# Moving the places at which SyncE hands over loads, in an attention kernel with a gated convolution

## Chip, cores, metric

The kernel runs on one core of a Trainium2 chip. The metric is the device time of one execution in microseconds (us), lower is better. Here PE is TensorE's matmuls and PEld its weight loads, DVE is VectorE, ACT ScalarE, POOL GpSimd and SP SyncE, which hands loads to the DMA engines.

## What is computed

For 8 batches of 8 heads there are 512 local and 32 global positions with head size 64. Global queries attend to all positions; a local query attends to the global ones and to local ones at most 32 away. The heads are joined into rows of 512, and a gated block follows: a causal convolution over 5 positions makes a gate, `w_val` a value, and `w_out` is applied to their product.

```
s_g  = scale * q_g @ k_all.T;            out_g = softmax(s_g) @ v_all
s_ll = where(|i - j| <= 32, scale * q_l @ k_l.T, -1e9)
out_l = softmax(concat(scale * q_l @ k_g.T, s_ll)) @ v_all
x = concat(out_g, out_l) as rows of 512
gate = sigmoid(sum_k conv_w[k] * x shifted by 4 - k)
out = (gate * (x @ w_val)) @ w_out
```

## The kernel before

Work is cut into 32 units of two heads (four units a batch). For unit u: `s` makes the scores of 16 blocks of 32 queries against 128 keys each (L521), `mx` masks them and takes the maximum (DVE), `exp` is on ACT, `t` transposes on PE (L554 or L262), `tc` copies to SBUF, `av` multiplies by v (L573), `eps` and `norm` divide, `xt` transposes again (L600 or L262), and `tap` and `conv` make the gate. `gs`, `gmax`, `gexp`, `gt`, `gav`, `gx` do the same for the global queries of a batch (L424, L476, L498). Of a batch, `g1` (L705) multiplies by `w_val` and `g2` (L733) by `w_out`, each matrix split in a high and a low part, so three matmuls of 512 columns for each step `g1.b.e.t` or `g2.b.r.e`. `w0` to `w7` are the weights' 128-row pieces, split in steps `s0` to `s7` on ACT and DVE.

The order of everything is written out by hand in one text, `ORDER` (L52 on): names in the order in which instructions are put into the program; a name's engine takes them in that order. Three kinds of names in it are loads on SyncE: `iqN` (q and k of unit N, 624 KB, L348), `ivN` (v of unit N, 975 KB) and `wiN` (weight piece, 512 KB). SyncE takes them in the order of the text, one queue.

A load's place matters beyond its rank in that queue. `on_pe` notes each TensorE instruction as it is put down, and `transfer` makes the load wait for the last one noted:

```
    def on_pe(ins):
        last_pe[:] = [ins.ins]

    def transfer(out, in_):
        ins = nc.sync.dma_start(out, in_).ins
        if last_pe:
            tc.add_manual_dep(ins, last_pe[0].name, after, reason="a load's place in the line")
```

So a load is handed to the DMA engines when the TensorE work named ahead of it has ended. There are four buffers for q/k and four for v; a load also waits for its buffer's last reader. The first thirteen loads (`FIRST`) are handed over at the start and aren't in `ORDER`.

Of the kernel before, what the change touches and what calls it, by code (L numbers as in the profile page):

```python
# [69 lines left out]
g1.0.3.2 sig3 exp8.1 eps7:ACT iv8 gv.0.2 g1.0.3.3 xt6T@4 norm7 gl.0.1 gv.0.3 gh.0.2:ACT t8@01 w7.s2 w7.s3 xc4:ACT  # L70
xc6:ACT tc8.0:ACT xt5T@6 w6.s7 gs2@24 xc5:ACT iv9 gmax2.0 gh.0.3:ACT gx1@0 gxc1:ACT w7.high:ACT w7.s4 g2.0.0.0@6 gmax2.1
gexp2.0 s9@07 w7.s5 w7.s6 gl.0.3 s10@23 iv11 tap6:ACT tc8.1:ACT gt2.0T@4 gl.0.2 xt7@1 g2.0.0.1 tap5:ACT w7.s7 xc7:DVE
xh7:ACT gtc2.0 tap4:DVE g2.0.0.2 g2.0.0.3 g2.0.1.0@1 g2.0.1.1 g2.0.1.2 ob.0.0:ACT tap7:ACT mx10.0 iq12 xl7 halo7:ACT
gexp2.1 g2.0.1.3 g2.0.2.0@2 g2.0.2.1 ob.0.1:ACT halo4:DVE av8@5 xh4:POOL gav2.0@1 conv4.0 xh6:ACT mx9.0 exp9.0 mx9.1
s11@07 xl4 conv4.1 iq13 xh5:DVE mx10.1 exp9.1 gt2.1T@3 g2.0.2.2 g2.0.2.3 iq14 eps8:DVE exp10.0 norm8 t9@56 mx11.0
halo5:DVE mx11.1 exp10.1 iq15 gtc2.1 tc9.1:DVE ob.0.2:ACT t10@04 gav2.1 tc9.0:ACT tc10.0:ACT conv4.2 av9@5 xl5
tc10.1:ACT geps2:ACT av10@3 gnorm2 st.0.1 gx2@1 g2.0.3.0@0 eps9:ACT conv5.0 conv4.3 eps10:ACT exp11.1 gxc2:ACT norm10
g2.0.3.1 g2.0.3.2 g2.0.3.3 exp11.0 xt8T@1 t11@73 xc8:ACT xl6 ob.0.3:ACT norm9 s12@65 iv14 conv5.1 conv5.2 tc11.0:ACT
s13@24 conv5.3 xt9@7 conv7.0 g1.1.0.0@0 mx13.0 exp13.0 iv12 g1.1.0.1 g1.1.0.2 g1.1.0.3 halo6:ACT xc9:ACT xh9:ACT mx13.1
mx12.0 mx12.1 sig4 gv.1.0 gs3@16 iq16 s14@05 exp12.0 gmax3.0 st.0.3 tc11.1:ACT halo8:DVE av11@3 xt10@1 gexp3.0 eps11:ACT  # L80
mx14.0 iv13 conv7.1 g1.1.1.0@0 iq17 norm11 g1.1.1.1 xc10:ACT tap8:ACT conv6.0 gmax3.1 exp12.1 g1.1.1.2 gt3.0T@3 conv6.1
gtc3.0 iv15 conv7.2 xt11T@6 t12@12 mx14.1 sig5 exp14.0 s15@34 tc12.1:DVE tc12.0:ACT g1.1.1.3 g1.1.2.0@2 conv6.2 exp13.1
gexp3.1 g1.1.2.1 gv.1.1 mx15.0 iq18 conv7.3 g1.1.2.2 conv6.3 g1.1.2.3 xc11:ACT g1.1.3.0@7 g1.1.3.1 mx15.1 sig6 exp14.1
gv.1.2 sig7 av12@3 gh.1.1:DVE st.0.2 gav3.0@0 gt3.1T@1 t13@65 gh.1.0:DVE eps12:DVE norm12 st.0.0 t14@34 gtc3.1 gl.1.0
# [957 lines left out]
```

## Time and profile before

| | before |
|---|---|
| three runs, median | 355.54 us (355.24 to 357.9) |
| profiled execution, its own time | 355.0 us |
| its span, first to last instruction | 353.2 us |
| mean granted TensorE clock | 0.990 |
| TensorE busy (matmuls) | 335.6 us, 95% of the span |
| VectorE busy | 309.0 us, 87% |
| ScalarE busy | 224.8 us, 64% |
| DMA queue of the loads (q1) | 57.01 MB |
| DMA queue of instructions (q8) | 52 packets, 0.85 MB |

The span is the part of the profiled execution from its first to its last instruction; 1.8 us lie around it. Times in the rows are counted from the span's start. "issue" as the cause of idle time means that the engine waited for nothing that the profile shows. Matmul ends are modelled, so a piece of the chain can start a few tenths after the last matmul did. A window counts the instructions that start in it.

### The profile page before, as it was taken

The page shows a single profiled execution, that of the slowest core. Times are in us where ns is not written, and L with a number is a line of the kernel's source. Part 1 is how long each engine was busy: PE and PEld are TensorE (multiplying, and loading weights), DVE is VectorE, ACT ScalarE, POOL GpSimd, SP SyncE. Part 2 cuts the span into 40 slices and gives each one's busy share as a digit, 9 for nine tenths or more (in the row PEclk, how much of TensorE's full clock was granted, in tenths as well). Part 3 has the DMA queues.
Part 4 walks back from the last instruction along what each step waited for, and adds up shares of the span by engine and source line. Part 5 has one row for each costly group of instructions (what it writes and reads, how often), then busy time and mean ns, then how long its engine had stood idle before and what let it go on. Part 6 is the DMA issues. An engine that isn't in the chain of part 4 may idle for free.

```text
span 353.2 us, 15341 instructions
## 1 busy us (share of the span) xinstructions
PE 335.6 (95%) x6658; PEld 269.3 (76%) x6658; DVE 309.0 (87%) x1035; ACT 224.8 (64%) x579; POOL 13.6 (4%) x23
## 2 busy tenths in 40 slices
PE   5889899999799999999999999999999999999994
PEld 2547678778577788788887878887888888888893
DVE  3799999999949999999999998899688898897981
ACT  2779799778728795965965458737876504434221
POOL 4014110001000000000000000000000000000000
PEclk9899999999989999999999999999999999999999
DMA  7987779674719936944494338543580110012124
GB/s 241 413 347 257 264 252 375 228 262 182 248 35 371 341 110 222 371 144 150 130 338 151 140 124 301 199 127 126 183 320 19 55 38 30 2 59 89 60 91 149
DMA packets 17107, 66.64 MB, mean 189 GB/s; under 512 B 1808, under 2 KB 3984, under 8 KB 17040
## 3 DMA queue, kind: packets, MB, share of 16 engines
q1 hardware_dynamic: 12240, 57.01, 45.6%
q10 hardware_dynamic: 4800, 8.65, 6.5%
q8 instruction: 52, 0.85, 0.9%
q14 instruction: 15, 0.12, 0.1%
HBM read 56.74 MB, written 8.91 MB: 186 GB/s over the span
## 4 chain that ended last, share of the span: by engine, by line
PE 88%; ACT 3%; DVE 3%; issue 2%; DMA 2%; ACTq 0%; SPq 0%
PE psum L705 27%; PE psum L733 26%; PE psum L521 9%; PE psum L573 9%; PE psum L262 7%; PE psum L476 3%; DMA qk<-in_qk_dram 2%; PE psum L600 2%; PE psum L424 2%; PE psum L554 2%; PE psum L677 1%; DVE wa L232 1%; ACT pm L540 1%; DVE wraw L232 1%; PE psum L498 1%
## 5 line engine op out<-in xcount | busy, mean ns | idle before, releaser
L232 DVE SCALAR_TENSOR_TENSOR gate<-xc,cw,gate 128x512 f32<-128x512 f32 x120 | 87.6, 750 | 1.0
L540 ACT ACTIVATE pm<-pm,mx 128x128 f32<-128x128 f32 x256 | 80.0, 392 | 9.4 <-DVE mx L232 9.4
L232 DVE CUSTOM_DVE_ANT_0 pm<-psum,small 128x128 f32<-128x128 f32 x256 | 57.8, 285 | 14.3 <-PE psum L521 14.2
L733 PE MATMUL psum<-wol,gh 128*128 128x512 f32 x128 | 50.8, 397 | 3.2 <-issue 3.2
L733 PE MATMUL psum<-woh,gh 128*128 128x512 f32 x128 | 52.1, 407 | 0.0
L705 PE MATMUL psum<-xh,wvh 128*128 128x512 f32 x128 | 52.1, 407 | 0.0
L733 PE MATMUL psum<-woh,gl 128*128 128x512 f32 x128 | 50.6, 395 | 0.0
L705 PE MATMUL psum<-xh,wvl 128*128 128x512 f32 x128 | 50.1, 392 | 0.0
L705 PE MATMUL psum<-xl,wvh 128*128 128x512 f32 x128 | 49.9, 390 | 0.0
L521 PE MATMUL psum<-qk 64*32 64x128 f32 x2048 | 36.5, 277 | 3.3 <-DMA qk<-in_qk_dram 3.3
L689 ACT ACTIVATE gate<-gate 128x512 f32<-128x512 f32 x32 | 19.8, 630 | 29.9 <-DVE gate L232 29.9
L521 PEld LDWEIGHTS psum<-qk 64*32 64x32 f32 x2048 | 29.3, 107 | 9.5 <-DMA qk<-in_qk_dram 5.2
L573 PE MATMUL psum<-v,pts 128*32 128x65 f32 x2048 | 34.5, 221 | 2.0 <-issue 1.8
L573 PEld LDWEIGHTS psum<-v,pts 128*32 128x32 f32 x2048 | 30.5, 110 | 7.3 <-issue 2.8
L330 ACT COPY pts<-psum 128x512 f32<-128x512 f32 x53 | 29.6, 585 | 5.6 <-DVE mx L232 2.4
L733 PEld LDWEIGHTS psum<-wol,gh 128*128 128x128 f32 x128 | 24.5, 191 | 8.1 <-issue 3.6
L733 PEld LDWEIGHTS psum<-woh,gh 128*128 128x128 f32 x128 | 24.7, 193 | 5.2 <-DVE gm L232 0.2
L733 PEld LDWEIGHTS psum<-woh,gl 128*128 128x128 f32 x128 | 24.5, 191 | 5.3
L705 PEld LDWEIGHTS psum<-xh,wvh 128*128 128x128 f32 x128 | 24.0, 188 | 5.8 <-DVE gv L232 0.3
L705 PEld LDWEIGHTS psum<-xh,wvl 128*128 128x128 f32 x128 | 24.0, 188 | 5.5 <-issue 0.3
L705 PEld LDWEIGHTS psum<-xl,wvh 128*128 128x128 f32 x128 | 24.1, 188 | 4.6 <-issue 0.2
L232 DVE SCALAR_TENSOR_TENSOR gv<-gate,psum 128x512 f32<-128x512 f32 x32 | 21.8, 683 | 5.5 <-PE psum L705 3.3
(124 smaller groups left out, 516.4 us busy)
## 6 DMA issues: line engine op xcount, KB each, us to landing
v<-in_vw_dram SPq DMA_DIRECT2D x32, 975.0 KB, 5.5
qk<-in_qk_dram SPq DMA_DIRECT2D x32, 624.0 KB, 5.3
out_dram<-ob ACTq DMA_DIRECT2D x32, 256.0 KB, 2.3
wraw<-in_w_val_dram SPq DMA_DIRECT2D x4, 512.0 KB, 12.1
wraw<-in_w_out_dram SPq DMA_DIRECT2D x4, 512.0 KB, 4.7
out_dram<-obg SPq DMA_DIRECT2D x4, 64.0 KB, 1.7
out_dram<-obg ACTq DMA_DIRECT2D x4, 64.0 KB, 2.0
small<-in_mask_dram SPq DMA_DIRECT2D x1, 148.0 KB, 3.3
```

Source lines behind the costliest of these rows:

```text
L232: ins = made(*args, **kwargs)
L262: on_pe(T.matmul(out, in_, ident[D * r:D * r + D, D * r:D * r + D], is_transpose=True, **more))
L330: A.copy(out, in_)
L424: on_pe(T.matmul(s[h][SG * c:SG * c + SG, cols], qkt[rows, SL + SG * h:SL + SG * h + SG], keys, start=True, stop=True))
L476: on_pe(T.matmul(ag[SG * c:SG * c + SG, :], pgt[:k, s, SG * c:SG * c + SG], vt[:k, w, h, :], start=(n == 0), stop=(n == len(steps) - 1)))
L521: on_pe(T.matmul((sx, sy)[h][32 * j:32 * j + 32, i, :], qkt[rows, 32 * m:32 * m + 32], qkt[rows, k0:k0 + P], start=True, stop=True))
L540: A.activation(out=pm[:, h, i, :], in_=pm[:, h, i, :], func=AF.Exp, bias=mx[:, c:c + 1], scale=-1.0)
L554: on_pe(T.transpose(pt[:, i, :], pm[:, h, i, :], ident))
L573: on_pe(T.matmul(ax[32 * j:32 * j + 32, h, E1 * i:E1 * i + E1], q, vt[:, block_win(4 * i + j), h, :], start=True, stop=True))
L689: A.activation(out=g, in_=g, func=AF.Tanh, scale=0.5)
L705: on_pe(T.matmul(box["pv", e], w[:, e, t * P:t * P + P], x, start=(t == 0 and q == 0), stop=(t == NDT - 1 and q == 2)))
L733: on_pe(T.matmul(box["po", r], g[:, e, rs], w[:, e, :], start=(e == 0 and q == 0), stop=(e == NDT - 1 and q == 2)))
```

## The change

Only `ORDER` changes. It holds 60 names of loads (`iq`, `iv`, `wi`), and 47 of them now stand at another place against TensorE's work: 22 earlier, 25 later. The names of all other work stand in the same order as before, so no instruction of PE, DVE, ACT or POOL is added, removed or moved against another of its engine. Some loads are now handed over together, and SyncE's own order changes in places. As an example, two lines of the text before and the lines that hold the same loads now:

```diff
-gav1.0@2 exp6.0 mx7.0 av5@4 iq10 sig0 gv.0.0 gt1.1@16 mx7.1 conv2.2 conv3.2 sig1 eps5:ACT exp7.0 norm5 gtc1.1 g1.0.1.2
-g1.0.1.3 t7.0@0 conv2.3 exp7.1 iq11 g1.0.2.0@1 w6.s0:ACT w6.s1 tc7.0:ACT gv.0.1 gh.0.0:ACT w6.s2 g1.0.2.1 t7.1@6 t6@54
+conv2.3 exp7.1 g1.0.2.0@1 w6.s0:ACT wi7 w6.s1 tc7.0:ACT iq10 gv.0.1 gh.0.0:ACT w6.s2 g1.0.2.1 t7.1@6 t6@54 conv3.3 w6.s3
+s8@03 tc6.1:ACT gav1.1 tc7.1:ACT av7@6 iq11 gh.0.1:ACT mx8.0 tc6.0:ACT sig2 mx8.1 iv10 geps1:DVE av6@4 w6.s4 w7.s0:ACT
```

Of the loads spoken of below, the TensorE work ahead of each (what it waits for), before and now:

| load | before, behind | now, behind |
|---|---|---|
| iv6, iv5, iv7 | pc1.4, g1.0.0.2, t4.0 | av2, s5, gs1 |
| iq10 | av5 | g1.0.2.0 |
| iq11 | t7.0 | av7 |
| iq13, iq14, iq15 | s11, g2.0.2.3, t9 | g2.0.1.2, g2.0.1.2, s11 |
| iq16, iv13 | gs3, xt10 | s14, t12 |
| iq27 | g1.3.1.1 | g1.3.3.3 |

SyncE's own queue, in the part from v7 or v5 (first row) to v10 (last row). `v_` and `qk_` are the buffers of a v or q/k load, `wraw_` that of a weight piece; the number behind a name counts what was made ahead of it in the program; the brackets name what the load waits for (PE: its place; DMAHW: an earlier transfer that shared its semaphore; Activation, DVE: its buffer). Before: v5, q/k 8, w6, w7, q/k 9, q/k 10, q/k 11, v10.

```order
L348 DMA v_956<-in_vw_dram 128x1950 [waits DMAHW6_49,PE_49]
L348 DMA qk_962<-in_qk_dram 128x1248 [waits DMAHW7_49]
L348 DMA wraw_1025<-in_w_out_dram 128x1024 [waits DMAHW0_49,PE_49,Activation_49]
L348 DMA wraw_1067<-in_w_out_dram 128x1024 [waits DMAHW1_49,DVE_49,PE_49]
L348 DMA qk_1072<-in_qk_dram 128x1248 [waits DMAHW2_49]
L348 DMA qk_1141<-in_qk_dram 128x1248 [waits DMAHW3_49,PE_49]
L348 DMA qk_1186<-in_qk_dram 128x1248 [waits DMAHW4_49,PE_49]
L348 DMA v_1319<-in_vw_dram 128x1950 [waits DMAHW5_49,PE_49]
```

Now v7, w6, q/k 8, q/k 9, w7, q/k 10, q/k 11, v10:

```order
L348 DMA v_902<-in_vw_dram 128x1950 [waits DMAHW6_49,PE_49]
L348 DMA wraw_1004<-in_w_out_dram 128x1024 [waits DMAHW7_49,PE_49,Activation_49]
L348 DMA qk_1016<-in_qk_dram 128x1248 [waits DMAHW0_49,PE_49]
L348 DMA qk_1137<-in_qk_dram 128x1248 [waits DMAHW1_49,PE_49]
L348 DMA wraw_1187<-in_w_out_dram 128x1024 [waits DMAHW2_49,PE_49,Activation_49]
L348 DMA qk_1191<-in_qk_dram 128x1248 [waits DMAHW3_49]
L348 DMA qk_1311<-in_qk_dram 128x1248 [waits DMAHW4_49,PE_49]
L348 DMA v_1324<-in_vw_dram 128x1950 [waits DMAHW5_49]
```

w7 has moved behind q/k 9; where no PE stands in the brackets, the load has the same place as the one ahead of it.

The same queue at the third of the places, from q/k 12 to v14. Before:

```order
L348 DMA qk_1625<-in_qk_dram 128x1248 [waits DMAHW1_49,PE_49]
L348 DMA qk_1750<-in_qk_dram 128x1248 [waits DMAHW2_49,PE_49]
L348 DMA qk_1779<-in_qk_dram 128x1248 [waits DMAHW3_49,PE_49]
L348 DMA qk_1818<-in_qk_dram 128x1248 [waits DMAHW4_49,PE_49]
L348 DMA v_2032<-in_vw_dram 128x1950 [waits DMAHW6_49,PE_49]
```

Now:

```order
L348 DMA qk_1586<-in_qk_dram 128x1248 [waits DMAHW1_49,PE_49]
L348 DMA qk_1619<-in_qk_dram 128x1248 [waits DMAHW2_49,PE_49]
L348 DMA qk_1629<-in_qk_dram 128x1248 [waits DMAHW3_49]
L348 DMA qk_1752<-in_qk_dram 128x1248 [waits DMAHW4_49,PE_49]
L348 DMA v_1958<-in_vw_dram 128x1950 [waits DMAHW6_49,PE_49]
```

The order is the same; each number is smaller, so each load stands further ahead in the program, and q/k 14 has the place of q/k 13.

## Rows read from the trace of the kernel before

**Rows 1.** The page's first part: span, then each engine's busy time.
```profile
span 353.2 us, 15341 instructions
PE 335.6 (95%) x6658; PEld 269.3 (76%) x6658; DVE 309.0 (87%) x1035; ACT 224.8 (64%) x579; POOL 13.6 (4%) x23
```
**Rows 2.** Chain that ended last, in order of time: start us, us, what.
```profile
39.79 0.95 issue
...
41.51 1.08 PE psum L521 x64
...
51.23 1.04 PE psum L573 x64
...
65.33 0.87 issue
66.20 1.90 PE psum L573 x107
...
78.95 6.16 PE psum L733 x27
...
91.69 1.82 PE psum L573 x128
...
94.69 3.21 issue
97.90 3.68 PE psum L733 x8
...
199.18 5.66 PE psum L705 x24
...
211.00 1.15 PE psum L424 x32
```
**Rows 3.** Timeline of DVE and PE: start us, us, engine line op, [idle before <-releaser].
```profile
104.60 0.29 DVE L232 CUSTOM_DVE_ANT_0 pm<-psum,small 128x128 f32<-128x128 f32 x1 [5.08 <-PE psum L521]
...
115.11 0.21 PE L262 MATMUL psum<-ident,pm 64*128 64x64 f32 x1 [0.34 <-issue]
```
**Rows 4.** Windows: us, busy of PE, PEld, DVE, ACT, POOL, clock, DMA, GB/s.
```profile
40.74:66.20 25.46, 24.59 (x638) 19.45 (x637) 24.64 (x102) 22.78 (x60) 1.75 (x2) 1.00 0.83 303
66.20:97.90 31.70, 28.49 (x764) 23.13 (x765) 30.08 (x106) 24.01 (x67) 1.75 (x2) 1.00 0.64 219
97.90:115.11 17.21, 16.87 (x382) 13.10 (x383) 11.54 (x56) 10.55 (x27) 0.00 (x0) 0.90 0.60 216
115.11:162.69 47.58, 47.58 (x1277) 39.15 (x1276) 45.39 (x173) 36.10 (x96) 0.00 (x0) 1.00 0.61 221
...
66.19:85.10 18.91, 18.89 (x379) 15.11 (x383) 18.07 (x62) 14.06 (x34) 1.75 (x2) 1.00 0.66 228
```
**Rows 5.** DMA queues over the span: queue, kind, packets, MB, share of 16 engines.
```profile
q8 instruction: 52, 0.85, 0.9%
```
**Rows 6.** Timeline of SyncE's queue: start of the first, time to the last's end.
```profile
57.02 4.18 SPq L348 DMA_DIRECT2D qk<-in_qk_dram  x3
...
87.87 3.00 SPq L348 DMA_DIRECT2D qk<-in_qk_dram  x3
```
**Rows 7.** DMA queues from 91.3 to 95.4 (q10, the stores, left out).
```profile
q1 hardware_dynamic: 257, 1.17, 87.2%
```
**Rows 8.** DMA queues from 95.4 to 96.5: the queue of instructions.
```profile
q8 instruction: 1, 0.02, 5.2%
```
**Rows 9.** DMA from 97.9 to 98.95, then the queue from 98.95 to 100.
```profile
DMA packets 0, 0.00 MB, mean 0 GB/s; under 512 B 0, under 2 KB 0, under 8 KB 0
...
q8 instruction: 1, 0.02, 5.7%
```
**Rows 10.** Window behind the third stop, columns as in rows 4.
```profile
98.00:101.00 3.00, 3.00 (x7) 2.41 (x8) 1.49 (x3) 0.00 (x0) 0.00 (x0) 0.50 0.02 5
```
**Rows 11.** DMA queues from 82.9 to 83.2: the queue of instructions.
```profile
q8 instruction: 1, 0.02, 19.4%
```
**Rows 12.** Accesses of the q/k buffers: their loads, from issue to landing.
```profile
DMA to landing us min/median/max: 3.6/5.3/12.6
```

More of the change, by code (lines that the diff above doesn't have):

```diff
@@ L59 @@
-tc3.0:ACT w4.s2 w4.s3 iq6 halo1 gexp0.1 tc3.1:ACT w4.s4 gav0.0@1 mx4.0 gt0.1T@4 pc1.0@2 w5.s0:ACT w5.s1 pco0:ACT w0.s7
-xl1 w4.s5 tc2.0:ACT w5.s2 pc1.1 pc1.2 gtc0.1 w3.high:ACT mx4.1 w4.s6 iq7 exp4.0 av3@4 exp4.1 eps3:ACT gav0.1 w3.s6
-geps0:ACT iv4 av2@6 w5.s3 eps2:ACT w4.high:ACT s5@30 norm3 xt3@4 gnorm0 t4.0@1 xc3:ACT norm2 w5.s4 iv7 gx0@5 pc1.3 mx5.0
+w1.s7 w0.high:ACT t3.0@4 w3.s4 t3.1@2 w3.s5 iq5 s4@76 w4.s0:ACT tc2.1:ACT dg1 w2.s6 w4.s1 w2.s7 xc1:ACT xh1:ACT
+tc3.0:ACT w4.s2 w4.s3 halo1 gexp0.1 iq6 tc3.1:ACT w4.s4 gav0.0@1 mx4.0 gt0.1T@4 pc1.0@2 w5.s0:ACT w5.s1 pco0:ACT w0.s7
@@ L62 @@
+xl1 w4.s5 tc2.0:ACT w5.s2 pc1.1 iq7 pc1.2 gtc0.1 w3.high:ACT mx4.1 w4.s6 exp4.0 av3@4 exp4.1 eps3:ACT gav0.1 w3.s6 iv4
+geps0:ACT av2@6 w5.s3 iv6 eps2:ACT w4.high:ACT s5@30 iv5 norm3 xt3@4 gnorm0 t4.0@1 xc3:ACT norm2 w5.s4 gx0@5 pc1.3 mx5.0
 xh3:POOL w4.s7 mx5.1 exp5.0 w5.s5 g1.0.0.0@3 w5.high:POOL tap3:ACT gxc0:ACT g1.0.0.1 halo3:ACT xt2@6 xn3 tc4.0:ACT pc1.4
-iv6 xc2:ACT conv3.0 xl3:ACT xh2:ACT fix0 t4.1@0 gs1@46 w5.s6 pco1:ACT tc4.1:ACT exp5.1 xl2 s6@21 tap2:ACT t5.0@0 w3.s7
-gmax1.0 gexp1.0 g1.0.0.2 tc5.0:ACT fix1 iv5 gmax1.1 gexp1.1 iq8 mx6.0 w2.high:ACT av4@4 w5.s7 t5.1@0 conv3.1 gt1.0@62
@@ L70 @@
[L70 to L84, printed above, removed]
@@ L150 @@
[L150 to L153 removed]
+xc2:ACT conv3.0 xl3:ACT xh2:ACT fix0 t4.1@0 gs1@46 w5.s6 pco1:ACT tc4.1:ACT exp5.1 xl2 iv7 s6@21 tap2:ACT t5.0@0 w3.s7
@@ new lines @@
+gnorm1 w6.s5 xt4@3 eps6:ACT gl.0.0 norm6 w6.s6 w7.s1 w6.high:POOL exp8.0 g1.0.2.2 g1.0.2.3 g1.0.3.0@2 g1.0.3.1 iv8
+g1.0.3.2 sig3 exp8.1 eps7:ACT gv.0.2 g1.0.3.3 xt6T@4 iv11 norm7 gl.0.1 gv.0.3 gh.0.2:ACT t8@01 w7.s2 w7.s3 xc4:ACT
+xc6:ACT tc8.0:ACT xt5T@6 w6.s7 gs2@24 xc5:ACT gmax2.0 gh.0.3:ACT gx1@0 gxc1:ACT w7.high:ACT w7.s4 g2.0.0.0@6 gmax2.1
+gexp2.0 s9@07 w7.s5 w7.s6 iv9 gl.0.3 s10@23 tap6:ACT tc8.1:ACT gt2.0T@4 gl.0.2 xt7@1 iq12 g2.0.0.1 tap5:ACT w7.s7
+xc7:DVE xh7:ACT gtc2.0 tap4:DVE g2.0.0.2 g2.0.0.3 g2.0.1.0@1 g2.0.1.1 g2.0.1.2 iq13 ob.0.0:ACT tap7:ACT mx10.0 iq14 xl7
@@ new lines @@
+halo7:ACT gexp2.1 g2.0.1.3 g2.0.2.0@2 g2.0.2.1 ob.0.1:ACT halo4:DVE av8@5 xh4:POOL gav2.0@1 conv4.0 xh6:ACT mx9.0 exp9.0
+mx9.1 s11@07 iq15 xl4 conv4.1 xh5:DVE mx10.1 exp9.1 gt2.1T@3 g2.0.2.2 g2.0.2.3 eps8:DVE exp10.0 norm8 t9@56 mx11.0
+halo5:DVE mx11.1 exp10.1 gtc2.1 tc9.1:DVE ob.0.2:ACT t10@04 gav2.1 tc9.0:ACT tc10.0:ACT conv4.2 av9@5 xl5 tc10.1:ACT
+geps2:ACT av10@3 gnorm2 st.0.1 gx2@1 g2.0.3.0@0 eps9:ACT conv5.0 conv4.3 eps10:ACT exp11.1 gxc2:ACT norm10 g2.0.3.1
+g2.0.3.2 iv14 g2.0.3.3 exp11.0 xt8T@1 t11@73 xc8:ACT xl6 ob.0.3:ACT norm9 s12@65 conv5.1 conv5.2 tc11.0:ACT s13@24
@@ new lines @@
+tc16.0:ACT s19@76 gt4.0T@3 tc16.1:ACT t17@51 t18@02 gtc4.0 tc18.0:ACT halo13:DVE av16@3 gav4.0@0 xh13:DVE mx19.0
+conv11.2 g1.2.1.0@7 mx19.1 sig9 tc17.1:ACT eps16:DVE tc17.0:ACT g1.2.1.1 g1.2.1.2 norm16 xt15T@3 xl13 gt4.1T@5
+tc18.1:ACT s20@12 conv10.2 conv10.3 gtc4.1 av17@5 iq23 xc15:ACT mx20.0 av18@3 conv14.2 gav4.1 conv12.1 eps17:ACT
+g1.2.1.3 iv20 g1.2.2.0@1 mx20.1 geps4:ACT st.1.0 conv11.3 norm17 halo15:ACT eps18:ACT g1.2.2.1 g1.2.2.2 g1.2.2.3 norm18
+gnorm4 gv.2.1 s21@06 xh14:DVE xl14 mx21.0 gh.2.0:DVE gs5@24 tap13:ACT mx21.1 gmax5.0 gl.2.0 sig10 exp20.1 xt17@7
@@ new lines @@
+conv21.2 tap20:ACT xh23:ACT mx27.1 gv.4.0 av26@4 eps26:DVE norm26 av25@1 gh.4.0:DVE s28@06 gl.4.0 conv20.0 conv18.3
+g1.4.1.0@5 conv19.3 sig18 exp27.0 mx28.0 sig19 iq30 g1.4.1.1 g1.4.1.2 g1.4.1.3 geps6:ACT eps25:ACT conv21.3 iq31
+g1.4.2.0@4 g1.4.2.1 g1.4.2.2 g1.4.2.3 g1.4.3.0@0 g1.4.3.1 conv20.1 mx28.1 gv.4.1 gv.4.2 g1.4.3.2 g1.4.3.3 norm25 exp27.1
+gh.4.2:ACT t27@41 gnorm6 gv.4.3 exp28.0 xt26T@5 tc27.0:ACT st.2.1 xh20:ACT gh.4.1:DVE xc26:DVE s29@27 gl.4.1 gl.4.2
+tc27.1:ACT gs7@53 halo23:ACT av27@0 iv28 mx29.0 gh.4.3:ACT gmax7.0 xh22:ACT eps27:ACT mx29.1 xt24@2 exp28.1 exp29.0
@@ new lines @@
+ob.4.3:ACT tc28.0:DVE st.4.3 mx31.1 av28@6 conv23.2 gav7.0@5 gv.5.0 tap25:ACT exp29.1 ob.4.2:ACT gt7.1T@1 gv.5.1
+conv25.0 exp31.1 eps28:ACT norm28 t30@43 t29@60 gtc7.1 t31@71 gh.5.0:DVE tc30.0:DVE tc30.1:ACT tc29.1:ACT tc31.0:ACT
+xt28T@3 g1.5.2.0@2 halo24:ACT tc29.0:ACT g1.5.2.1 g1.5.2.2 conv25.1 g1.5.2.3 g1.5.3.0@6 conv22.2 conv22.3 sig22 g1.5.3.1
+conv23.3 sig23 g1.5.3.2 tc31.1:ACT st.3.2 xc28:ACT xh26:ACT g1.5.3.3 gh.5.1:DVE gv.5.2 av30@2 gl.5.0 gh.5.2:DVE
+eps30:ACT gl.5.1 av29@0 xh27:DVE xl27 norm30 gav7.1 tap26:DVE xh25:ACT gv.5.3 gl.5.2 eps29:ACT gh.5.3:ACT av31@2
@@ new lines @@
+g1.6.2.0@3 gh.6.1:ACT g1.6.2.1 g1.6.2.2 xh30:ACT g1.6.2.3 gl.6.1 g1.6.3.0@1 g1.6.3.1 gh.6.0:ACT gl.6.0 gv.6.2 xl30
+gh.6.2:ACT gl.6.2 g1.6.3.2 g1.6.3.3 xt31@3 g2.6.0.0@7 gxc7:ACT gv.6.3 halo30:ACT g2.6.0.1 halo28:DVE gh.6.3:DVE gl.6.3
+g2.6.0.2 g2.6.0.3 xc31:ACT xh31:ACT g2.6.1.0@3 g2.6.1.1 g2.6.1.2 g2.6.1.3 g2.6.2.0@1 g2.6.2.1 g2.6.2.2 g2.6.2.3
+g2.6.3.0@5 halo31:DVE conv30.0 conv30.1 xl31 conv28.0 tap31:ACT g2.6.3.1 ob.6.1:ACT st.6.1 g2.6.3.2 conv31.0 ob.6.0:DVE
+conv31.1 conv31.2 st.6.0 conv28.1 ob.5.1:ACT conv30.2 xc29:ACT xh29:DVE halo29:DVE xl29 conv31.3 tap29:ACT conv29.0
@@ new lines @@
+g2.7.1.3 g2.7.2.0@6 g2.7.2.1 g2.7.2.2 g2.7.2.3 g2.7.3.0@4 g2.7.3.1 g2.7.3.2 g2.7.3.3 g1.g.0.0@2 gxl1 sigg1 g1.g.0.1
+g1.g.0.2 g1.g.0.3 g1.g.1.0@1 ob.7.1:DVE gconv3 st.5.0 ob.6.3:ACT st.6.3 ob.7.0:ACT st.7.1 g1.g.1.1 g1.g.1.2 g1.g.1.3
+gconv0 g1.g.2.0@3 g1.g.2.1 g1.g.2.2 sigg0 gv.g.0 gh.g.0:DVE g1.g.2.3 g1.g.3.0@0 gv.g.1 g1.g.3.1 gh.g.1:DVE sigg3 gl.g.0
+g1.g.3.2 g1.g.3.3 gl.g.1 g2.g.0.0@2 gv.g.2 gh.g.2:ACT gl.g.2 g2.g.0.1 g2.g.0.2 gv.g.3 gh.g.3:ACT gl.g.3 g2.g.0.3
+ob.g.0:ACT st.g.0 st.7.0 ob.7.3:ACT st.7.3 g2.g.1.0@1 g2.g.1.1 g2.g.1.2 ob.7.2:DVE g2.g.1.3 ob.g.1 st.7.2 st.g.1
```

128 lines of the change are left out of this document (54 added, 74 removed).

## Prediction, made before the changed kernel ran

> **What bounds the kernel now.** The page's first part is read first [rows 1]: TensorE is busy 95% of the span and VectorE 87%, so a gain must come out of TensorE's 17.6 us of idle time, or out of time in which it runs slowly. The chain of waits names the idle pieces that lie on the path [rows 2]: three pieces called "issue", 0.95, 0.87 and 3.21 us, in which TensorE waited for no semaphore. A fourth, shorter one is in the timeline at 115.11 [rows 3].
>
> What ends these stops is found by counting. Between the ends of successive stops the windows show 638 + 637, 764 + 765, 382 + 383 and 1277 + 1276 matmuls and weight loads [rows 4], in its first four rows; the last of these stretches ends at a small gap at 162.69. With the few wait-only instructions, which windows leave out, these are 5, 6, 3 and 10 times 256. The DMA table shows 52 packets, 0.85 MB, of kind "instruction" on a queue of their own, q8 [rows 5]: 16 KB each, and 13,316 matmuls and weight loads over 52 is 256. So one packet carries 256 TensorE instructions, and TensorE stops at the end of such a page when the next has not arrived.
>
> The largest stop shows why it is late. SyncE hands over three q/k loads from 87.87 to 90.86 [rows 6]. TensorE runs the page ahead of the stop from about 91.5 (its 128 matmuls and their weight loads are the 1.82 us at 91.69 [rows 2]). From 91.3 to 95.4 the DMA engines are 87% busy with the loads and move no instruction packet [rows 7]; the packet comes in the next window, where its 5.2% of 16 engines for 1.1 us is 0.92 us of one engine [rows 8]. TensorE goes on at 97.90, 1.5 us after that window closes. With nothing ahead of it a fetch is quick: after 97.90 no packet moves for 1.05 us, and then one does [rows 9]. So 1.1 + 0.9 + 1.5 = 3.5 us from request to use, and behind loads as much longer as they take.
>
> The stop costs twice. From 98 to 101 the granted clock is 0.50, the lower of its two levels (1.2 of 2.4 GHz), after TensorE had stood for 3.2 us [rows 10]; in the windows on either side of the 0.87 us stop the mean is 1.00 [rows 4].
>
> The Trainium skill (DMA: Bandwidth & Descriptors, section Queues, rings and completion order) says that each DMA engine takes turns between its queues at every packet; by that the fetch would have waited for less than a microsecond and not for three loads, and this trace disagrees with its four microseconds. The Trainium skill (Runtime: NRT & Kernel Launch, section Instruction fetch mechanics) calls the cost of a 16 KiB block "mostly hidden"; the trace agrees on the block and, at these stops, disagrees on the hiding.
>
> **The change part by part.** No instruction of TensorE, VectorE or ScalarE is added, removed or moved, so the pages end at the same instructions. Each load is handed over when the TensorE work written ahead of it has ended, so its new time is read off the old trace at that work's end.
>
> *Third stop (94.7).* Loads 13 and 14 of q/k go from 87.8 and 89.8 to the end of g2.0.1.2, which is 18 of the 27 matmuls of the row at 78.95 [rows 2], so 83.1; load 15 goes from 90.5 to the end of s11 at 87.8. Two loads of 624 KB from 83.1 on take about 5 us, the third ends by 91.5; nothing stands ahead of a fetch asked for at 91.3 to 91.5. It lands 3.5 us later, at 94.8 to 95.0, and not at 97.9: **3.0 us**, with a stop of about 0.4 us left. The clock then stays up: the eight matmuls after the stop took 3.68 us, where 27 of the same line take 6.16, 0.228 each [rows 2], so 1.82: **1.9 us**.
>
> *Second stop (65.3).* Before, three q/k loads stood at 57.02 to 61.20 [rows 6], ahead of the fetch for the page that the stop waits for. TensorE asks for a page before it begins the one ahead of it: a fetch starts between 82.9 and 83.2 [rows 11] at a place that TensorE reaches at 85.1, three pages after the second stop (379 + 383, the last of [rows 4]); so that request went out near 82, 3 us or less ahead. The page that runs into the second stop begins near 62.7, and its request falls near 60.6. After the change load 9 stands ahead of it at 58.3 and lands in time; load 10 goes to 61.5, behind the request, and load 11 to the end of av7, inside the 1.90 us of matmuls that follow the stop [rows 2]. **0.9 us**.
>
> *Fourth stop (115.1).* Load v13 goes from 111.5 to 115.3, behind the stop, and q/k 16 from 108.9 to 109.9, after the request. **0.3 us** [rows 3].
>
> *First stop (39.8).* The two q/k loads that stand ahead of its fetch stay where they were: nothing is gained.
>
> *What it may cost.* v6 and v5 move from 47.5 and 51.2 to 41.5 and 42.6, right behind v4 at 39.4; 41.5 is the end of av2, where the L521 row begins [rows 2]. Three loads of 975 KB at the 303 GB/s of that stretch [rows 4] take about 9.9 us from 40.4 and end near 50.3. The fetch asked for at about 46 then lands at 52.7 at worst; the page that needs it begins two pages after the first stop, at 51.5, in the L573 piece at 51.23 [rows 2]. Price: nothing if the fetch passes one of the three, 1.2 us if it waits for all; I take 0.3, since the largest stop's fetch waited to the end of what was queued, but a packet needs only its own DMA engine. Loads that come later have less room, the smallest being 6.2 us (q/k 27, from 192.9 to the end of the L705 row at 199.18, 204.8; needed at 211.00 [rows 2]), over the median landing of 5.3 [rows 12]: nothing. Behind a load that waits in SyncE's queue stand only other loads.
>
> *Who is late next.* VectorE. From 66.2 to 97.9 it is busy 30.08 of 31.70 us and from 115.1 to 162.7 45.39 of 47.58 [rows 4]. But it stood idle for 5.08 us up to 104.60, waiting for the scores that TensorE's stop delayed [rows 3]. So VectorE can follow by 5.08 us plus the 1.62 it idled from 66.2 to 97.9: at most 6.7, at least 5.1. I take 0.2 us lost to it.
>
> Sum: 3.0 + 1.9 + 0.9 + 0.3 = 6.1, less 0.3 and 0.2: **5.6 us**. Against the profiled execution's own 355.0 us (span 353.2 and 1.8 around it) that is 349.4. The median of the runs shown, 355.54, lies 0.5 higher; 5.6 off it is 349.9. I forecast **349.7**, and 348.6 to 351.4 for this case by the bounds (VectorE lets 5.1 to 6.7 pass; the early fetch takes 0 to 1.2).
>
> **The rivals.**
> *A new stop takes part of it back.* The bunched loads (v4, v6, v5 at 39 to 43; q/k 16 and v15 near 110) hold a fetch longer than I think, or VectorE lets less through. For it: every stop so far came from loads in a row. Against: after the second page of loads there are 4 us to spare. A new stop of 1.2 us takes 1.2; one of 3 us at the lower clock as well takes 4.9. Time 351.4 to 354.5.
> *The moves change no fetch.* Were the fetch late for another reason than the loads ahead of it (its own memory, its own queue), it would come at the same instruction as before, and all is as it was: 355.0 to 355.5. Against: the fetch after 97.90 came in 1.1 us with the loads gone [rows 9]. The two rules of the Trainium skill cited above would give this case.
> *Slower: a load is late.* q/k 27 now has 6.2 us. If it lands later than that, TensorE stands at 211; the longest landing of such a load is 12.6 us [rows 12], so up to 6.4 us of stop and, after a stop longer than 3 us, 1.9 us at the lower clock: 8.3 - 5.6 = 2.7 slower, 358.2. It decides at 6.2 us. Against: no other load is handed over with it, and the shortest landing is 3.6 us.
>
> **How the numbers follow.** My case 0.66, a part given back 0.20, no change 0.08, slower 0.05, more than 6.7 us gained 0.01. The time is my case's. A measurement of this kernel tells apart about 1%, 3.6 us: faster means under 352.0. That is my case, the 0.01 and 0.06 of the partial one: 0.73. Same: 0.14 of the partial case, 0.07 of no change: 0.21. Slower: 0.06. The range reaches down to 348.6, and up into the partial case, to 353.2: it leaves out 0.05 of that case, 0.08, 0.05 and a little of mine, about 0.2.
>
> **What would show it.** In the changed profile the issue pieces of 0.87 and 3.21 us are gone from the chain, the one of 0.95 at 39.8 is still there, and a piece of some 0.4 us may stand near 93. No 3 us stretch at 0.50 clock around 95 to 101; VectorE's 5.08 us idle before the mx of unit 13 is under 1 us. The windows between the stops left are still multiples of 256. A new issue piece near 51 would be the price of v6 and v5. The forecast is wrong if the 3.21 us piece is still there with the DMA engines idle ahead of it, or if VectorE's idle time goes but TensorE's waits for VectorE grow by as much.

## The result, and the profile after

The changed kernel takes **350.79 us** (median, 350.07 to 351.7) against 355.63 us before: ratio 0.985, with an interval of 0.980 to 0.990, so 3.6 to 7.0 us less. The forecast was 349.7, its range 348.6 to 353.2. Beside later runs of before it stood at 0.987 and 0.990. Ratios are taken over the executions that lie no more than 1.5% above the fastest of the same kernel. The profiled execution has a span of 349.3 us, 3.9 less than the one of before.

The page's first part and the queue of instructions, after (they answer [rows 1] and [rows 5]):

```profile
span 349.3 us, 15339 instructions
...
PE 334.7 (96%) x6658; PEld 270.0 (77%) x6658; DVE 308.5 (88%) x1035; ACT 225.6 (65%) x579; POOL 13.5 (4%) x23
...
q8 instruction: 52, 0.85, 0.9%
```

TensorE does the same work and fetches the same 52 pages. What went is 3.0 us of idle time (17.6 became 14.6) and 0.9 us of busy time. The chain that ended last, after (start us, us, what; it answers [rows 2]):

```profile
28.66 5.61 DMA qk<-in_qk_dram
...
41.00 0.91 PE psum L573 x64
41.91 1.09 PE psum L521 x64
...
93.50 2.90 PE psum L733 x12
...
124.71 0.63 issue
```

The issue pieces of 0.95, 0.87 and 3.21 us are gone. In the place of the third stop the L733 matmuls run through: twelve take 2.90 us, where eight took 3.68 behind the stop. Three pieces are new: a q/k load that TensorE waits for, an issue piece at 124.7, and a wait for v18, which the timeline below shows.

Windows after (us, busy of each engine, clock, DMA share, GB/s): the stretch from the place of the third stop to that of the fourth, and its first 3 us.

```profile
94.27:109.37 15.10, 15.10 (x383) 11.94 (x383) 14.28 (x60) 11.71 (x33) 0.00 (x0) 1.00 0.66 211
...
94.30:97.30 3.00, 3.00 (x41) 2.30 (x48) 2.93 (x6) 2.14 (x8) 0.00 (x0) 1.00 0.29 50
```

Three pages ran in 15.10 us with no idle time, against 17.21 in [rows 4], and there the clock is 1.00, with no stretch as in [rows 10]. The fetch that was late now has no load beside it; only a store's packets move with it. DMA queue of instructions after, from 91.9 to 93 us:

```profile
q8 instruction: 1, 0.02, 5.7%
```

Timeline after: what stood idle, and what ended it.

```profile
34.32 0.95 PE L521 MATMUL psum<-qk 64*32 64x128 f32 x49 [0.95 <-DMA qk<-in_qk_dram]
...
82.84 5.09 SPq L348 DMA_DIRECT2D qk<-in_qk_dram  x3
...
99.42 0.29 DVE L232 CUSTOM_DVE_ANT_0 pm<-psum,small 128x128 f32<-128x128 f32 x1 [0.16 <-PE psum L521]
...
125.34 0.81 PE L573 MATMUL psum<-v,pts 128*32 128x65 f32 x41 [0.63 <-issue]
...
150.03 0.76 PE L476 MATMUL psum<-v,pgt 96*32 96x65 f32 x36 [0.29 <-DMA v<-in_vw_dram]
```

VectorE's idle 5.08 us ahead of unit 13's mask [rows 3] are 0.16. Three waits took their place in part: for q/k 4 at 33.4, for a page at 124.7, for v18 at 149.7.

Where the time went is seen by comparing the start of the same matmul in the two profiled executions:

| matmul | before | changed | difference |
|---|---|---|---|
| a transpose in the head (L554), ahead of every moved load | 18.89 | 19.97 | +1.07 |
| first of s4 (L521), which needs q/k 4 | 32.23 | 34.32 | +2.08 |
| first behind the first stop (L573) | 40.74 | 41.22 | +0.47 |
| first behind the second stop (L573) | 66.20 | 65.77 | -0.43 |
| first behind the third stop (L733) | 97.90 | 94.27 | -3.63 |
| seven matmuls later (L733) | 101.05 | 96.00 | -5.05 |
| first behind the fourth stop (L262) | 115.11 | 109.37 | -5.74 |
| behind the new stop (L573) | 130.05 | 125.34 | -4.71 |
| gav4.0 (L476), which needs v18 | 154.19 | 150.03 | -4.16 |
| behind the gap at 162.69 (L705) | 162.69 | 158.89 | -3.81 |

From there on the two run alike to the end, within 0.2 us. The first row is no effect of the change but of the clock. Ahead of that transpose the same 64 matmuls are 1.12 us of the chain before and 1.95 us after (the first line is from before):

```profile
14.88 1.12 PE psum L521 x64
...
14.97 1.95 PE psum L521 x64
```

From 15.0 to 18.3 the granted clock was 1.00 before and 0.50 after. In two further profiles of the changed kernel it was 1.00 and 0.58 there, and the transpose starts at 19.2 and 20.3. All fourteen profiles of this document fall into two sets: in seven these matmuls take 1.2 us by the timeline and the transpose starts at 18.8 to 19.6, in seven they take 1.8 to 2.0 us and it starts at 19.9 to 20.6. The three profiles of the changed kernel lie in both sets. So the two profiles compared here understate the change: counted from that transpose, the changed kernel gained 5.0 us to the last matmul and not 3.9. It is also why the mean granted clock is 0.990 in both, although the slow stretch behind the third stop is gone.

### The profile page after: what moved, and what is told of

Same layout as the page of the kernel before. It is cut to its first block, busy times and chain, and to the rows that moved or that the text cites. A ratio compares the mean times of both kernels' runs of the same rounds, so it can differ in the third digit from the quotient of the medians.

```text
span 349.3 us, 15339 instructions
## 1 busy us (share of the span) xinstructions
PE 334.7 (96%) x6658; PEld 270.0 (77%) x6658; DVE 308.5 (88%) x1035; ACT 225.6 (65%) x579; POOL 13.5 (4%) x23
## 4 chain that ended last, share of the span: by engine, by line
PE 88%; DMA 6%; ACT 2%; DVE 1%; issue 1%; ACTq 0%; SPq 0%; DVEq 0%
PE psum L705 27%; PE psum L733 26%; PE psum L521 10%; PE psum L573 9%; PE psum L262 6%; DMA qk<-in_qk_dram 4%; PE psum L476 3%; DMA v<-in_vw_dram 3%; PE psum L600 2%; PE psum L424 2%; PE psum L677 2%; PE psum L554 2%; ACT pm L540 1%; PE psum L498 1%; DVE pm L232 0%
## 5 line engine op out<-in xcount | busy, mean ns | idle before, releaser
L705 PE MATMUL psum<-xh,wvh 128*128 128x512 f32 x128 | 51.8, 405 | 0.0
L733 PE MATMUL psum<-woh,gh 128*128 128x512 f32 x128 | 51.7, 404 | 0.0
L705 PE MATMUL psum<-xh,wvl 128*128 128x512 f32 x128 | 50.2, 392 | 0.1
L733 PE MATMUL psum<-wol,gh 128*128 128x512 f32 x128 | 50.1, 391 | 0.0
L733 PE MATMUL psum<-woh,gl 128*128 128x512 f32 x128 | 50.0, 391 | 0.0
L705 PE MATMUL psum<-xl,wvh 128*128 128x512 f32 x128 | 49.9, 390 | 0.0
L521 PE MATMUL psum<-qk 64*32 64x128 f32 x2048 | 37.5, 285 | 4.7 <-DMA qk<-in_qk_dram 4.6
L521 PEld LDWEIGHTS psum<-qk 64*32 64x32 f32 x2048 | 30.5, 110 | 10.1 <-DMA qk<-in_qk_dram 6.2
L573 PEld LDWEIGHTS psum<-v,pts 128*32 128x32 f32 x2048 | 31.1, 111 | 6.0 <-issue 1.6
L573 PE MATMUL psum<-v,pts 128*32 128x65 f32 x2048 | 34.9, 223 | 0.7 <-issue 0.6
L705 PEld LDWEIGHTS psum<-xh,wvh 128*128 128x128 f32 x128 | 24.1, 188 | 6.3 <-DVE mx L232 0.7
L705 PEld LDWEIGHTS psum<-xh,wvl 128*128 128x128 f32 x128 | 24.0, 188 | 5.7 <-issue 0.5
L733 PEld LDWEIGHTS psum<-woh,gh 128*128 128x128 f32 x128 | 24.4, 191 | 5.1 <-DVE gm L232 0.2
L733 PEld LDWEIGHTS psum<-woh,gl 128*128 128x128 f32 x128 | 24.0, 188 | 5.2
L733 PEld LDWEIGHTS psum<-wol,gh 128*128 128x128 f32 x128 | 24.1, 188 | 4.7 <-issue 0.3
L705 PEld LDWEIGHTS psum<-xl,wvh 128*128 128x128 f32 x128 | 24.1, 188 | 4.3
```

What stands on the lines that cost most here:

```text
L521: on_pe(T.matmul((sx, sy)[h][32 * j:32 * j + 32, i, :], qkt[rows, 32 * m:32 * m + 32], qkt[rows, k0:k0 + P], start=True, stop=True))
L573: on_pe(T.matmul(ax[32 * j:32 * j + 32, h, E1 * i:E1 * i + E1], q, vt[:, block_win(4 * i + j), h, :], start=True, stop=True))
L705: on_pe(T.matmul(box["pv", e], w[:, e, t * P:t * P + P], x, start=(t == 0 and q == 0), stop=(t == NDT - 1 and q == 2)))
L733: on_pe(T.matmul(box["po", r], g[:, e, rs], w[:, e, :], start=(e == 0 and q == 0), stop=(e == NDT - 1 and q == 2)))
```

## The experiments

Four groups of kernels, each beside before on one chip. Medians of before there were 356.4 to 357.3 us, a microsecond above the first runs, so ratios are compared and not times.

| kernel | ratio to before | interval |
|---|---|---|
| third stop alone (from before) | 0.988 | 0.982 to 0.993 |
| q/k 13 to 15 back | 0.998 | 0.993 to 1.002 |
| q/k 15 back | 0.989 | 0.984 to 0.994 |
| q/k 4 back | 0.989 | 0.983 to 0.995 |
| changed, again | 0.987 | 0.983 to 0.991 |
| q/k 18, 19 later | 0.985 | 0.981 to 0.989 |
| five places | 0.991 | 0.988 to 0.995 |
| half a page | 1.064 | 1.057 to 1.071 |
| all stops | 0.983 | 0.978 to 0.988 |
| second half | 0.984 | 0.979 to 0.988 |
| second half, again | 0.987 | 0.981 to 0.993 |
| changed, third time | 0.990 | 0.984 to 0.995 |

**The third stop alone.** To the kernel before only the changed kernel's places around the third stop are given (v8, v9, v11 and q/k 12 move likewise, one or two steps each). In the edits below each line is one name of `ORDER`, the unmarked ones are the work between the loads, and `...` stands for names left out:

```diff
 g2.0.1.2
+iq13
...
 mx10.0
-iq12
+iq14
...
 s11
+iq15
...
 conv4.1
-iq13
...
 g2.0.2.3
-iq14
...
 exp10.1
-iq15
```

> The kernel before, with only the loads around the third stop moved to the changed kernel's places: v8, v9, v11 and q/k 12 to 15. All other loads stay. Theory (the fetch waits for the loads handed over ahead of it): the stop at 94.7 shrinks from 3.21 us to 0.3 or less and the half-speed stretch behind it goes, 3.0 + 1.7 us; the stops at 39.8, 65.3 and 115.1 stay. Time 355.6 - 4.7 = 350.9 us. Rival 1 (VectorE is the bound behind the stop and lets less through): VectorE's idle 5.08 us ends as waits of TensorE for VectorE, time 352 to 354. Rival 2 (the moves change no fetch; the gain came from elsewhere): 355.6.

Measured: ratio 0.988, 4.4 us less (2.5 to 6.3). Over all twelve of its executions the median is 353.96 us, 3.2 less than before's 357.18. The profiled execution has a span of 353.2 us, so only its stops and waits are read. Chain:

```profile
40.80 0.47 issue
66.15 1.15 issue
96.51 0.67 issue
```

Windows (columns as above), the 3 us behind the third stop:

```profile
97.20:100.20 3.00, 3.00 (x40) 2.32 (x48) 2.90 (x6) 1.31 (x4) 0.00 (x0) 1.00 0.03 5
```

The second stop, whose loads were not moved, is still there; the third is 0.67 us, more than the 0.3 expected, and the clock behind it stays up. So the moves around the third stop are worth most of the gain by themselves. Rival 1 would have given 1.6 to 3.6 us, and the time alone does not rule it out; the waits do. From 60 to 340 us TensorE had no wait for VectorE of 0.2 us or more. What took a part back was a load that had not moved, a v load for which TensorE, now earlier, waited:

```profile
121.40 0.76 PE L476 MATMUL psum<-v,pgt 96*32 96x65 f32 x34 [1.51 <-DMA v<-in_vw_dram]
```

**The three loads put back.** The changed kernel with

```diff
 g2.0.1.2
-iq13
...
-iq14
...
 s11
-iq15
...
 conv4.1
+iq13
...
 g2.0.2.3
+iq14
...
 exp10.1
+iq15
```

> The changed kernel with only q/k 13, 14 and 15 put back behind the TensorE work they had before. Theory: the three loads stand ahead of the fetch again, the stop near 94 comes back at 3.0 to 3.4 us with the half-speed stretch behind it, and nothing else changes: 350.8 + 3.0 + 1.7 = 355.5 us. Rival (the gain needs the other moves as well, or comes from them): 351 to 353.

Measured: 0.998, so of the gain nothing is left that can be told from zero (-0.6 to 2.4 us). Its chain, from the third stop on:

```profile
94.76 3.04 issue
129.61 0.50 issue
```

DMA queues from 91.4 to 95.5 (there is no q8 row), and the window behind the stop:

```profile
q1 hardware_dynamic: 260, 1.16, 86.3%
```

```profile
98.00:101.00 3.00, 3.00 (x8) 2.01 (x7) 1.55 (x3) 0.00 (x0) 0.00 (x0) 0.53 0.11 18
```

Three loads of sixty undo the change: the engines are 86% busy with loads, no page moves, TensorE stops for 3 us and then runs at the lower clock, as in [rows 7] and [rows 10]. The rival (the gain needs the other moves, or comes from them) would have left 2.6 to 4.6 us, above the interval.

**One load put back.** Only q/k 15 goes behind t9 again:

```diff
 s11
-iq15
...
 exp10.1
+iq15
```

> The changed kernel with only q/k 15 put back: one load ahead of the fetch and not three, handed over about 1 us before the fetch is asked for at 91.1. Theory: the fetch starts at the end of this one load on its DMA engine, 93.3 to 94.1 instead of 91.98, lands at 95.7 to 96.5, and the stop (0.24 us in the changed kernel) is 1.7 to 2.5 us. Whether the clock falls after a stop of that size no row shows so far (not after 0.87 us, yes after 3.21): 352.6 us if it does not, 354.3 if it does. Rival (turns at every packet): the fetch starts within a microsecond, 350.8.

Measured: 0.989; against the changed kernel's 0.985 to 0.990 the time alone shows no loss. The profile shows it. Timeline of SyncE, the chain, and the DMA queues from 91.7 to 93.9 and from 94.0 to 95.1:

```profile
90.92 0.33 SPq L348 DMA_DIRECT2D qk<-in_qk_dram  x1
```

```profile
95.08 1.29 issue
```

```profile
q1 hardware_dynamic: 122, 0.59, 88.6%
...
q8 instruction: 1, 0.02, 5.0%
```

One load, handed over 1.0 us before TensorE comes to the page ahead, holds the fetch until 94.08, and TensorE goes on at 96.36. That is inside the 95.7 to 96.5 that was expected for a wait behind one load. The stop is 1.29 us by the chain (1.7 between the starts of the matmuls around it), smaller than the three loads' 3.04 and larger than the 0.5 at most that the changed kernel shows here in three profiles. The clock did not fall:

```profile
96.30:99.30 3.00, 2.94 (x32) 2.25 (x32) 2.91 (x5) 0.72 (x3) 0.00 (x0) 1.00 0.20 34
```

The delay grows with the loads ahead. Counting 256 instructions back from the stop, TensorE came to the page ahead at 91.9, and the fetch began 2.2 us later. With all three loads ahead it began 4.0 us later (before) and 3.9 (the run above). In the ten other profiles, half a page left out, it began after 0.7 to 1.3.

The Trainium skill (DMA: Bandwidth & Descriptors, section Queues, rings and completion order) says that a DMA engine drains a whole packet, typically about 9 to 17 descriptors, from one queue before it turns to another. The records of the trace are of single rows (122 of them make 0.59 MB above), and the 128 rows of a q/k load make 8 for each of 16 engines. If a row is one descriptor, one load's share may be a single packet of that rule, and the wait behind one load does not contradict it. So the prediction's "less than a microsecond" does not follow from the rule, and whether the traces disagree with it stays open: how much of the loads a packet holds no run shows.

**q/k 4.** The changed kernel with w4 and q/k 4 where they were:

```diff
 s3
+wi4
...
 w2.s5
-wi4
+iq4
...
 av1
-iq4
```

> The changed kernel with w4 and q/k 4 put back to their places before. In the changed kernel TensorE waits 0.95 us at 33.4 for q/k 4, which is handed over 1.05 us of TensorE work later than before and lands after 5.3 us; but the first stop (0.95 us at 39.8) is gone. Theory (one hides the other: TensorE held up at 33.4 reaches the page's end 1 us later, the fetch is no earlier): the wait at 33.4 goes, the stop near 40 comes back at 0.9 to 1.2 us, time 350.8 as it was, within 0.4. Rival (the late load is a loss of its own): 349.8.

Measured: 0.989, as the changed kernel. Timeline:

```profile
33.89 1.16 PE L521 MATMUL psum<-qk 64*32 64x128 f32 x64 [0.39 <-DMA qk<-in_qk_dram]
...
41.54 0.76 PE L573 MATMUL psum<-v,pts 128*32 128x65 f32 x36 [0.53 <-issue]
```

The wait for q/k 4 falls to 0.39 us and the first stop is back, with 0.53 and not the 0.9 expected. From the head to the last matmul this execution took 324.2 us, the changed kernel's first 324.4, which fits the wait and the stop cancelling. It is not shown: the interval is over 4 us wide, so the time does not rule out the rival's 1 us, and in two other profiles the wait and the stop stand together. With the three loads put back, whose head is the changed kernel's, TensorE waited 0.62 us for q/k 4 and then stopped for 0.97; with all stops mended (below), q/k 4 is in its old place, and the two are 0.84 and 0.81.

**The changed kernel again, twice.**

> The changed kernel as it is, beside the next kernels on the same chip and profiled a second time: 4 to 5 us under before (350.8 against 355.6). All theories expect the same; it shows how far stops of the same kernel differ from profile to profile: the small one near 124.7 and the wait for q/k 4 at 33 should be there again, the stops at 65 and 95 not.

> The changed kernel beside it: 351 us, 0.986 of before; the stops near 124.7 (0.84 and 1.12 us so far) and 158.4 and the wait for v18 near 150 again.

The first of these, by the chain and the timeline:

```profile
125.29 1.12 issue
159.39 0.55 issue
```

```profile
51.68 0.77 PE L573 MATMUL psum<-v,pts 128*32 128x65 f32 x40 [0.31 <-issue]
```

In the third profile none of these stands as a piece of 0.3 us or more, while the wait for q/k 4 was larger:

```profile
35.18 1.09 PE L521 MATMUL psum<-qk 64*32 64x128 f32 x60 [1.44 <-DMA qk<-in_qk_dram]
```

So the expectation failed in its detail: the stop at 125 came in two profiles of three, the wait for v18 in one (in the third, TensorE waited 0.48 us at 118.5 for another v load), the wait for q/k 4 in all (0.95, 0.67, 1.44). The stops at 65 and the 3 us stop at 95 came in none.

**q/k 18 and 19.** The fetch whose page is missing at 124.7 starts late because the one ahead of it stood behind q/k 18:

```diff
 exp14.0
 iq17
-iq18
...
 st.0.2
-iq19
+iq18
...
 xc12:ACT
+iq19
```

> The changed kernel with q/k 18 handed over behind gav3.0 (where q/k 19 was) and q/k 19 behind g1.1.3.3. In the changed kernel the fetch that starts at 119.13 stands behind q/k 18 and lands at 121.5; the next fetch starts only at 123.06, and TensorE stops 0.84 us at 124.7. Theory (a fetch waits for the loads ahead of it, and the next one is asked for only when it has landed): with q/k 18 behind its request the first of the two starts near 117.2, the second near 121, and the stop goes: 350.8 - 0.8 = 350.0 us. Rival (VectorE and ScalarE leave TensorE no room there, waits of 0.05 to 0.4 us of slack at a dozen places): the stop goes, the time stays 350.8.

Measured: 0.985, the changed kernel beside it 0.987: the intervals overlap, the time does not decide it. In the trace the stop is gone, and from the head to the last matmul this execution took 323.0 us, the changed kernel's three 324.4, 326.3 and 324.9. One trace does not decide it, since the changed kernel's third has no stop there either. Over the runs of all sections, the fetch ahead began 2.2 to 3.7 us after TensorE had come to the page before in the six profiles with q/k 18 at the changed kernel's place, and the stop was 0 to 1.12 us; in the five with q/k 18 at the new place they are 0.7 to 2.2 and 0 to 0.41.

**Half a page.** A test of what the stops are, which moves the page ends and no load:

```diff
         keep_clock(2, 7, zf)
+        for _ in range(32):
+            on_pe(T.matmul(psum[:32, 7, :8], zf[:, :32], zf[:, :8], start=True, stop=True))
```

> The changed kernel with 32 tiny float32 matmuls (128 instructions of TensorE, half a page) put in while TensorE waits for its first q/k load. No load moves against the work and the results of these matmuls are not used; only the ends of all pages come 128 instructions earlier in the work. Theory (pages of 256 instructions, and each load's place fits the request of one fetch): the loads now stand just ahead of requests and not behind them, and stops of 1 to 4 us come at many page ends, the largest where several loads stand in a row (near 104, 117, 205): at least 8 us longer, 359 or more; each stop 128 instructions ahead of a page end of the changed kernel. Rival (the gain came from the loads' own times and not from the fetches): 350.8 to 351.5, stops where they were.

Measured: **1.064**, 378.85 us, 27 us longer than the changed kernel beside it. The 64 passes themselves lie under the wait for the first q/k load (timeline):

```profile
5.14 3.58 PE L968 MATMUL psum<-zf 128*32 128x8 f32 x64
8.66 0.68 PE L521 MATMUL psum<-qk 64*32 64x128 f32 x16
```

Behind the head the chain has thirteen issue pieces of 0.5 us and more, 22.7 us in all. The largest did not come where they were expected (near 104, 117 and 205). Among them:

```profile
41.49 2.72 issue
...
83.73 2.57 issue
101.49 1.44 issue
116.18 1.89 issue
149.28 3.23 issue
...
230.29 3.36 issue
```

Windows between the ends of such stops count TensorE's instructions:

```profile
86.30:102.93 16.63, 15.19 (x382) 12.46 (x382) 13.81 (x67) 11.79 (x33) 1.13 (x1) 1.00 0.60 204
102.93:118.07 15.14, 13.24 (x384) 10.42 (x383) 11.76 (x55) 9.62 (x27) 0.00 (x0) 1.00 0.56 177
118.07:152.51 34.44, 31.12 (x766) 25.07 (x767) 31.26 (x109) 26.39 (x71) 0.00 (x0) 0.95 0.61 217
...
152.51:378.00 225.49, 211.28 (x3441) 174.40 (x3441) 183.64 (x533) 117.64 (x294) 0.00 (x0) 0.99 0.37 130
```

The same count in the changed kernel, from the stop that ends at 125.34:

```profile
125.34:351.00 225.66, 218.99 (x3760) 181.02 (x3760) 195.65 (x584) 126.32 (x318) 0.00 (x0) 1.00 0.40 142
```

764, 767 and 1533 are 3, 3 and 6 pages but for the few wait-only instructions. (A window also counts an instruction that only runs over its edge; at the end of a stop there is none.) From 152.51 to the end 6882 are left, in the changed kernel 7520 from 125.34. The difference, 638, is two and a half pages but for two: the page ends do lie half a page off in the work. No load moved against the work, no result of these matmuls is used, and the kernel lost more than five times what the change had gained. The rival, that the loads' own times carry the gain, is out.

**Mending the places that the profile shows.**

> The changed kernel with the places mended that its profile shows as bad: q/k 4 ahead of w4 (TensorE waited 0.95 us for it at 33.4), q/k 6 behind the request of the fetch at 36.4 (first stop), q/k 18 and 19 as in the run that moves only these, v18 and v19 ahead of q/k 21 and 22 (v18 landed at 149.5, 0.55 us too late for gav4.0), and q/k 22 behind the request at 150.5 (stop of 0.47 at 158.4). Theory: 0.95 + 0.2 at the head, 0.8, 0.5, 0.3: 350.8 - 2.7 = 348.1 us. Rival (VectorE lets no more through): 349.5 to 350.5. The other way: q/k 22 or v19 in its new place holds a fetch and a stop of up to 1 us comes near 158: 349.

Its edit beside that of q/k 18 and 19:

```diff
 w2.s5
-wi4
+iq4
...
 av1@6
-iq4
+wi4
...
 gexp0.1
-iq6
...
 gt0.1T@4
+iq6
...
 halo14:DVE
-iq21
+iv19
...
 exp17.0
-iq22
+iv18
...
 ob.1.2:ACT
-iv19
-iv18
+iq21
...
 g1.2.1.0@7
+iq22
```

Measured: 0.991, no gain. Timeline of ScalarE:

```profile
32.49 0.71 ACT L290 ACTIVATE wa<-wraw 128x512 f32<-128x512 f32 x1 [1.19 <-DMA wraw<-in_w_out_dram]
```

w4, now behind q/k 4, came 1.19 us too late for ScalarE, which takes its work in order; the copies queued behind the split of w4 came late, and TensorE waited 1.0 and 0.5 us for ScalarE. Behind 100 us no issue piece above 0.3 us was left, and TensorE gained 1.9 us on the first profile of the changed kernel between 109 and 159. So two more kernels: that second half alone, and all places with the head mended in another way (w4 and q/k 4 as before; q/k 6 behind gt0.1, v5 behind g1.0.0.1, q/k 14 behind s11, q/k 15 behind gav2.1).

> The changed kernel with twelve loads moved: q/k 18, 19, 21, 22 and v18, v19 as in the run of five places, whose second half had none of the stops left; w4 and q/k 4 back to their places before (with w4 behind q/k 4, ScalarE waited 1.2 us for w4 and TensorE 1.6 for ScalarE); q/k 6 behind gt0.1 and v5 behind g1.0.0.1, each just behind the request of a fetch that it now stands ahead of (stops at 40 and 51, up to 0.75 and 0.5); q/k 14 behind s11 and q/k 15 behind gav2.1 (stops of 0.3 to 0.8 at 91 and 95). Theory: 0.85 + 0.55 + 0.4 in the second half, 0.5 to 1 in the first: 351 - 2.5 = 348.5 us, 0.979 of before. Rival: the moves trade places with other stops as at the head before: 350 to 351.

> The changed kernel with only q/k 18, 19, 21, 22 and v18, v19 moved, as in the run of five places; the head as in the changed kernel. Theory: the stop at 124.7 (0.84), the wait for v18 at 149.5 (0.55) and the stop at 158.4 (0.4) go: 351 - 1.8 = 349.2 us, 0.982 of before. Rival (VectorE takes a part back): 350 to 351.

All stops: 0.983, where 0.979 was expected. Its chain shows stops at the head again, larger than in the changed kernel, so the rival held there:

```profile
40.59 0.81 issue
52.35 0.76 issue
...
125.36 0.41 issue
```

Second half: 0.984, where 0.982 was expected, with 0.2 us of TensorE waiting for issue in the whole span and 322.8 us from the head to the last matmul.

> The kernel with q/k 18, 19, 21, 22 and v18, v19 moved, once more and beside the changed kernel on one chip. Its first profile had no stop over 0.3 us between 100 and 345 us; behind the first 20 us it took 322.8 us to the last matmul, the changed kernel 324.4 and 326.3 in its two profiles. Theory: 1.5 to 2 us below the changed kernel, 349.2. Rival (the fetches' own scatter from execution to execution outweighs the places): within 0.5 us of it.

Again: 0.987, 324.8 us from the head, with a stop of 0.40 at 126.5; the changed kernel beside it 0.990. Over all their runs the medians are 351.0 us (12 runs) and 351.7 (16). The order is the one expected, the 0.6 us is not told apart from the scatter, and no version here is shown to beat the changed kernel.

## Why the prediction was right, point by point

**Third stop, 3.0 us, and the clock, 1.9.** Right, the clock's part somewhat less: 3.2 us by the table (from -0.43 to -3.63), and 1.4 up to the start of the eighth matmul behind it (to -5.05). Put back, the loads brought both back (3.04 us, clock 0.53); alone, they gave most of the gain. The stop left over, expected at 0.4, is below 0.3 in the first profile, 0.4 and 0.5 in the others.

**Second stop, 0.9.** Right: 0.9 (from +0.47 to -0.43). No run moves its loads alone; where they stay, in the run of the third stop alone, the stop stays. **Fourth, 0.3.** By the table 0.7 went up to there, 0.34 of it the stop itself. The four gains make 6.2 us, the prediction's were 6.1.

**First stop, "stays where it was", and "the smallest room is 6.2 us (q/k 27)".** This step failed. The smallest room was that of q/k 4: its place moved by one TensorE step, from the end of s3 to the end of av1 (26.5 to 27.5 in the trace of before), and s4 needs it at 32.2; 4.7 us are less than the median landing of 5.3 [rows 12], and it landed after 5.6 by the chain. TensorE waited 0.67 to 1.44 us for it in three profiles. In these three the first stop, which was to stay, was gone, so the time hardly noticed. Whether the wait let that fetch catch up is open: with q/k 4 back the stop was back, but with the three loads back wait and stop stood together. q/k 27, the load on which the slower rival hung, kept nobody waiting.

**v6 and v5, 0.3 us.** Right in size: a stop of 0.3 at 51.4 in one profile of the changed kernel, none in two.

**VectorE, 0.2 us.** It let everything pass: 5.08 us idle became 0.16, and no wait of TensorE for VectorE grew to a piece of the chain.

**What the sum lacked** is the rival of a part taken back, in small: the fetch behind q/k 18 (1.0 us at 124.7 by the table), v18 (0.55), the gap at 158 (0.35), in the first profile. Its price was put at 1.2 to 4.9 us; it was 1.9 in the first profile and less in the third. With the 1.07 us that the clock cost in the head and the 0.6 us gained from there to the first stop, -6.2 + 1.9 + 1.07 - 0.6 is -3.8, the 3.9 us between the two profiles but for rounding. The medians differ by 4.8, near the 5.0 counted from the head. That the forecast came within 1.1 us is in part luck: 1.9 us were given back where 0.5 had been taken off, and against that stand the 0.6 up to the first stop, which the sum put at nothing.

## What to carry to other kernels

An engine that stops with nothing to wait for may be out of instructions: count its instructions between such stops, and if they come in multiples of one number, look at which transfers stand ahead of its fetches. A load's place then has two sides, its own due time and the fetch that it stands ahead of; hand a load over just behind a fetch's request, and keep the list of rooms complete, since the load that was overlooked is the one that cost. Whoever adds or removes instructions ahead of such a tuned order moves every page end: 128 instructions put into idle time cost this kernel 27 us, so places have to be found again after every edit.
